# Twelve idle products, four slots for attention's inputs, and 350 GB/s in the ordering

## The chip, the cores and the metric

The kernel runs on one core of a Trainium2 chip. The metric is the device time of one execution in microseconds (us); less is better. Three executions of the kernel before took 841.60, 839.25 and 843.16 us, median 841.6.

## What is computed

Retention attention (a causal product without softmax, weighted by a decay for each head) feeds two feed-forward networks in a row. All inputs are f32 or f64, and the result is f32:

```
scores = q @ k.T / 8                       # 4 batches, 8 heads, 576 tokens, 64 wide
ret    = scores * gamma[h] ** (i - j)      # for i >= j, else 0
x      = (ret @ v), heads joined           # 2304 tokens x 512
h      = max(x @ w_in, 0);  x = (h*h) @ w_out          # 512 -> 2048 -> 512
out    = ((x @ w_a) * (x @ w_b)) @ w_out2              # 512 -> 1536 -> 512
```

The weights are 64-bit floats, which the kernel takes as pairs of 32-bit words and turns into f32 on the chip.

## The kernel before, in words

**Attention** (`attention`) runs in 20 units: for each batch four units of one pair of heads (seven blocks of 64 tokens each) and a fifth with the last two blocks of all four pairs. A unit's loads (`Unit.load`, DMA issued by SP) bring q and k into a slot of the ring `qkr` and v and k into a slot of `vr`, 448 KB each for most. A ring has `SLOTS[tag]` slots; a load into a slot waits for the last reader of the unit that had it. ScalarE scales k (`tv`, L615). A small table `vt` comes over ScalarE's own queue; one copy of a tile `first` on ScalarE (L594) stands behind it. `products` issues three steps per unit on TensorE: states (`tv`, `vr`), scores (`qkr`), and for the unit before it the sums (`pt`, `vr`, `qkr`, `sa`). All are f32 products of 64x64 tiles, 28 instructions for a step of 14 products: one f32 product is two MATMUL records. VectorE masks the scores and scans the states, ScalarE copies them.

**The MLPs** run on f32r halves: every f32 operand is split in a high and a low part, and three products are summed (hi*hi, lo*hi, hi*lo), 384 or 448 columns each. The first four chunks of the first network are done while attention is still under way (`mlps`: `up` and `down` steps, mixed with attention's units); the rest follows with a Strassen-like scheme of seven products (`rest`). Weights go from DRAM to a raw tile (`wraw`, or a part of `xt` lent for it), through two conversions on ScalarE and four on VectorE (`convert`), and most back to DRAM (`kept`). `bank` names the eight PSUM banks: `up` uses bank 7, only its second step uses bank 3, which is also the fourth accumulator of `down`.

**The order of the work** is written by a planner (`Plan`, L63 to L231). Every step is added with its engines and their costs in ns, the keys that it reads and writes, and a function that emits it. `order` first gives each step a latest time from the running sum of TensorE's costs (`ideal`), then runs twelve rounds of a greedy simulation forward (`forward`: on each free engine the ready step with the least latest time begins, at once if there is one) and one backward that renews the latest times. The best round's sequence is emitted, and each engine, SP's DMA queue too, then works through its own instructions in that order on the chip; a wait blocks what is behind it on its engine. Three numbers of the model matter here: a transfer costs its bytes divided by 310 per ns (at least 620 ns, `dmac`) on one single resource, free from 600 ns on, and lands 2100 ns later; TensorE's costs count double before `COLD` = 9000 ns; and a step with a choice of VectorE or GpSimd is never begun on GpSimd. The function on top (`tile_retention_two_mlps`) fills the constant tiles on VectorE, adds the steps and emits them.

Of the kernel before, what the change touches and what calls it, by code (L numbers as in the profile page):

```python
# [11 lines left out]
F32 = mybir.dt.float32  # L12
# [10 lines left out]
P = 128  # L23
# [19 lines left out]
RUN, LAG = {1: 2, 2: 3}, {1: 1, 2: 2.5}  # L43
SEVENS = {(2, 0): [range(6, 12)], (2, 1): [range(0, 6), range(6, 12)], (2, 2): [range(0, 6), range(6, 12)], (1,0):[range(8,12)], (1,1):[range(8,12)], (1,2):[range(8,12),range(12,16)]}
AFTER = 0.0
SPAN = 0.8
MORE = (2, 0, 6)
PARTS = set()
# [2 lines left out]

WP, WE, RAWS = 2, 1, 2
SLOTS = dict(
    g=2, r=2, gh=2, qkr=3, vr=3, tv=2, pt=2, sa=2, wraw=2, ys=4,
)

ROUNDS = 12
# [5 lines left out]
class Plan:  # L63
# [3 lines left out]


    LAT = {"PE": 200, "DMA": 2100, "ACT": 160, "DVE": 150}
    COLD = 9000  # L70

    def __init__(self):
        self.steps = []
        self.writers, self.readers, self.users, self.before = {}, {}, {}, {}
        self.pe = 0.0

    def add(self, engines, fn, r=(), w=(), extra=(), lag=None):


        n = len(self.steps)  # L80
        deps = set(extra)
        for k in {k[:2] for k in (*r, *w)}:
            deps.update(self.before.get(k, ()))
            self.users.setdefault(k, []).append(n)
        for k in r:
            deps.update(self.writers.get(k, ()))
        for k in w:
            deps.update(self.writers.get(k, ()))
            deps.update(self.readers.get(k, ()))
        for k in w:  # L90
            self.writers[k], self.readers[k] = [n], []
        for k in r:
            if k not in w:
                self.readers.setdefault(k, []).append(n)
        ideal = None
        if "PE" in engines:
            self.pe += engines["PE"]
            ideal = self.pe

        locks = not any(k[0] == "bank" for k in r)  # L100
        self.steps.append((engines, fn, deps, ideal, locks, lag))
        return n
# [40 lines left out]
    def forward(self, late):  # L143

        n = len(self.steps)
        missing = [len(s[2]) for s in self.steps]
        ready_at = [0.0] * n
        ready = {e: [] for e in self.ENGINES}
        free = {e: 0.0 for e in self.ENGINES}
        free["DMA"] = 600.0  # L150
        coming = [(0.0, i) for i in range(n) if not missing[i]]
        spans, out = [None] * n, []
        now = 0.0
        while True:
            began = []
            while coming and coming[0][0] <= now:
                _, i = heapq.heappop(coming)
                for e in self.steps[i][0]:
                    heapq.heappush(ready[e], (late[i], i))
                if not self.steps[i][0]:  # L160
                    began.append((now, i, None))
            for e in self.ENGINES:
                while ready[e] and free[e] <= now:
                    _, i = heapq.heappop(ready[e])
                    if spans[i] is None and not (e == "POOL" and "DVE" in self.steps[i][0]):
                        cold = e == "PE" and now < self.COLD
                        free[e] = now + self.steps[i][0][e] * (2 if cold else 1)
                        spans[i] = now, free[e], e
                        began.append((free[e], i, e))
                        break  # L170
            for end, i, e in began:
                if e is None:
                    spans[i] = now, now, None
                out.append((now, i, e))
                for j in self.follow[i]:
                    ready_at[j] = max(ready_at[j], end + self.lag(i, e, j))
                    missing[j] -= 1
                    if not missing[j]:
                        heapq.heappush(coming, (ready_at[j], j))
            times = [t for t in free.values() if t > now]  # L180
            if coming:
                times.append(max(coming[0][0], now))
            if not times:
                break
            now = min(times)
        assert len(out) == n, (len(out), n)
        return out, now, spans
# [54 lines left out]
def tile_retention_two_mlps(  # L242
# [12 lines left out]
    V, A, G, T = nc.vector, nc.scalar, nc.gpsimd, nc.tensor  # L255
    plan = Plan()

    def mm(o, l, r, start, stop):
        T.matmul(o, l, r, start=start, stop=stop, skip_group_check=True)  # L259
# [10 lines left out]
    def add(o, a, b):  # L270
        return lambda e: eng[e].tensor_add(o(), a(), b())  # L271
# [5 lines left out]
        return lambda e: nc.sync.dma_start(out=o(), in_=i())  # L277

    def dmac(bytes_):
        return {"DMA": max(620.0, bytes_ / 310.0)}  # L280

    big = ctx.enter_context(tc.tile_pool(name="big", bufs=1))
    dram = ctx.enter_context(tc.tile_pool(name="dram", bufs=1, space=bass.MemoryType.DRAM))
# [2 lines left out]
    bank = [psum.tile([P, 512], F32, name=f"bank{i}") for i in range(8)]  # L286
# [26 lines left out]
    ap = st.enter_context(tc.tile_pool(name="attn", bufs=1, side="right"))  # L313
# [22 lines left out]
    V.memset(fade[:, :, ::LONG], 0.0)  # L336

    V.memset(mask, 1.0)
    first = ap.tile([P, 2], F32, name="first")
    V.memset(first, 0.0)  # L340

# [123 lines left out]
    def keep_pair(ph, c, src):  # L465

        w, kw = slot("wp")
        a, b = [kw + (0,)], [kw + (1,)]
        convert(lambda: w[:, 512:1536], a + b, src, 1024)
        combine(w, add, 0, 4, 5, b, a)  # L470
        combine(w, sub, 1, 0, 2, [], a)
        combine(w, sub, 4, 2, 4, a, b)
        combine(w, sub, 6, 3, 1, a, b)
        keep((ph, c, 0), lambda: w[:, :1024], a, 1024)
        keep((ph, c, 1), lambda: w[:, 1024:1792], b, 768)

    def keep_outs(ph, c, src):

        w, kw = slot("wp")
        a, b = [kw + (0,)], [kw + (1,)]  # L480
        convert(lambda: w[:, 512:1536], b, src, 1024)
        if any(c in r for k, rs in SEVENS.items() if k[0] == ph for r in rs):
            combine(w, add, 0, 3, 5, b, a)
            combine(w, sub, 6, 2, 3, b, a)
            combine(w, sub, 1, 0, 2, b, a)
            combine(w, sub, 7, 4, 1, b, a)
            keep((ph, c, 4), lambda: w, a + b, 2048)
        else:
            keep((ph, c, 4), lambda: w[:, 512:1536], b, 1024)
# [437 lines left out]
    def rest():  # L927
# [113 lines left out]
        for ph in (1, 2):  # L1041
            for p in range(PASSES):
# [3 lines left out]
                while cs:  # L1046
                    run = next((list(r)[::2] for r in sevens if cs[0] in r), None)
                    if run:
                        run = [c + i for c in run[::1 - 2 * (p % 2)] for i in range(2)]
                        k = max(at[ph, p, c] for c in run if (ph, p, c) in at) + 1  # L1050
                        jobs.append(("sevens", ph, p, run, len(run) * 21 / 12, k + AFTER, None, cs[0] == begin))
                        cs = cs[len(run):]
# [17 lines left out]
        for x, job in enumerate(jobs):  # L1070
            nxt = jobs[x + 1][5] if x + 1 < len(jobs) else job[5] + 99
            if job[0] == "sevens":
                jobs[x] = job[:6] + (min(nxt, job[5] + SPAN * len(job[3]) / (2 if job[1] == 1 else 1)),) + job[7:]
            elif job[6] > nxt:
# [72 lines left out]
        def group(unit, banks, fresh):  # L1147
# [11 lines left out]
            for i, q, s, b, start in PRODUCTS:  # L1159
# [26 lines left out]
                elif i == 4:  # L1186
                    c12, k12 = take(tfree)
                    plan.add({"DVE": dve(n)}, add(c12, lambda: o[2], p5), [ko[2], k5], [k12])
                    tfree.append((p5, k5))
                    if ph == 2:  # L1190
                        plan.add({"DVE": dve(n)}, mul(c12, c12, c22), [k22], [k12])
                        tfree.append((c22, k22))
                    else:
                        relu({"ACT": act(n)}, c12, k12, c12, k12)
                        square((ph, p, 1, c), c12, k12)
                elif i == 5:
                    c22, k22 = take(tfree)
                    plan.add({"DVE": dve(n)}, add(c22, lambda: o[3], p5), [ko[3], k5], [k22])
                    if ph == 1:
                        relu({"ACT": act(n)}, c22, k22, c22, k22)  # L1200
                        square((ph, p, 1, c + 1), c22, k22)
                elif ph == 2:
                    plan.add({"DVE": dve(n)}, mul(c11, lambda: o[3], c11), [ko[3]], [k11])
                    for j, (g, kg) in enumerate(((c11, k11), (c12, k12))):
                        if unit in sevened:
                            made[ph, p, j, c] = g, kg
                            continue
                        gh, kgh = take(gfree)
                        plan.add({"ACT": act(n)}, copy(lambda gh=gh: gh()[:, 0], g), [kg], [kgh + (0,)])
                        lower((ph, p, j, c), gh, kgh, g, kg)  # L1210
                else:
                    c21, k21 = take(tfree)
                    relu(pa, c21, k21, lambda: o[3], ko[3])
                    square((ph, p, 0, c + 1), c21, k21)
# [201 lines left out]
        for _ in downs:  # L1416
            pass

    att = attention()
    while env["done"] < READY[0]:  # L1420
        next(att)
# [86 lines left out]
```

## Time and profile before

| | |
|---|---|
| median of three executions | 841.6 us (839.25 to 843.16) |
| the profiled execution | 843.72 us, of which the span from first to last instruction is 842.0 us |
| TensorE matmul (PE) busy | 823.7 us, 98% |
| VectorE (DVE) busy | 760.7 us, 90% |
| ScalarE (ACT) busy | 592.2 us, 70% |
| mean granted clock of TensorE | 0.994 |
| moved by DMA | 165.48 MB, mean 197 GB/s |

A view of stretches gives, for each stretch in us from the span's start: its length, then for each engine the busy time and the number of instructions (x), the granted TensorE clock (1.00 is 2.4 GHz, 0.50 is 1.2 GHz), the busy share of the DMA engines and GB/s. PEld is the load of stationary operands, which overlaps PE. The view of waits gives engine, operand and line, what ended the wait, and total us, times, longest us; "issue" means that the profile shows nothing that was waited for. The timeline gives start, us, engine, line, operation, out<-in, tile, count, and in brackets the idle time before it and what ended that. Line 259 is the helper that issues every product, line 277 the one that issues every DMA on SP. q8 is a DMA queue of the kind "instruction". A few per cent of the matmul records can be missing.

### The profile page before, as it was taken

The numbers are of one execution on the slowest core, as the hardware profiler recorded it, in microseconds if no ns is written. First come the engines' busy times: TensorE is split into PE (matmuls) and PEld (weight loads), VectorE is DVE, ScalarE is ACT, GpSimd is POOL, SyncE is SP. The second block draws the span as 40 slices with busy tenths as digits, with TensorE's granted clock in tenths as the row PEclk, the third lists the DMA queues.
The fourth block names the chain that finished last, engine by engine and source line by source line (L and its number), as shares of the span: only waits on it lengthen the run. The fifth ranks groups of instructions, "written<-read, shape, count | busy, mean of one in ns | idle before, by whom it ended". The sixth has DMA issues, their size and how long they took to land.

```text
span 842.0 us, 16895 instructions
## 1 busy us (share of the span) xinstructions
PE 823.7 (98%) x6516; PEld 801.0 (95%) x6516; DVE 760.7 (90%) x1280; ACT 592.2 (70%) x1074; POOL 0.7 (0%) x6
## 2 busy tenths in 40 slices
PE   6799999999999999999999999999999999999998
PEld 6687888999999999999999999999999999999998
DVE  7898899979999999999999999999887798797777
ACT  5687769788977798778985667566566566566554
POOL 0000000000000000000000000000000000000000
PEclk9899999999999999999999999999999999999999
DMA  8878958897437772586345688624544324544324
GB/s 284 307 248 271 333 195 331 300 335 241 134 138 276 256 256 75 204 293 223 102 144 193 216 289 301 213 65 136 172 136 136 109 63 127 174 139 139 106 73 130
DMA packets 67713, 165.48 MB, mean 197 GB/s; under 512 B 7216, under 2 KB 32048, under 8 KB 64560
## 3 DMA queue, kind: packets, MB, share of 16 engines
q1 hardware_dynamic: 67488, 164.39, 58.4%
q8 instruction: 51, 0.84, 0.4%
q14 instruction: 30, 0.25, 0.1%
q10 hardware_dynamic: 144, 0.01, 0.0%
HBM read 126.88 MB, written 37.49 MB: 195 GB/s over the span
## 4 chain that ended last, share of the span: by engine, by line
PE 91%; DVE 3%; DMA 2%; ACT 2%; issue 1%; ACTq 0%; DVEq 0%
PE bank L259 91%; DVE w L268 1%; DMA w<-kept 1%; DMA qkr<-qk 1%; DMA vt<-vtab 0%; ACT wp L390 0%; DVE xt L271 0%; ACT we L416 0%; ACT tv L615 0%; DVE wp L409 0%; ACT xb L265 0%; ACT w L265 0%; DVE wp L268 0%; ACT bank L265 0%; DVE wp L420 0%
## 5 line engine op out<-in xcount | busy, mean ns | idle before, releaser
L259 PE MATMUL bank<-xo,w 128*128 128x384 f32 x1946 | 395.8, 334 | 0.9 <-ACT bank L265 0.9
L259 PEld LDWEIGHTS bank<-xo,w 128*128 128x128 f32 x1946 | 342.2, 188 | 1.8 <-ACT bank L265 1.6
L259 PE MATMUL bank<-xb,w 128*128 128x384 f32 (+3 forms) x918 | 200.9, 347 | 0.8 <-ACT r L845 0.8
L268 DVE TENSOR_TENSOR w<-w 128x512 fp32r<-128x512 f32 (+3 forms) x193 | 166.7, 872 | 11.6 <-ACT w L265 11.1
L265 ACT CAST w<-w 128x512 fp32r<-128x512 f32 (+3 forms) x193 | 145.9, 769 | 37.8 <-DMA w<-kept 37.6
L259 PEld LDWEIGHTS bank<-xb,w 128*128 128x128 f32 x918 | 163.1, 189 | 8.1 <-ACT r L845 1.2
L259 PE MATMUL bank<-gh,w 128*128 128x384 f32 (+3 forms) x606 | 135.8, 349 | 0.4 <-ACT bank L265 0.4
L259 PEld LDWEIGHTS bank<-gh,w 128*128 128x128 f32 x606 | 107.8, 188 | 7.3 <-ACT bank L265 0.7
L265 ACT COPY bank<-bank 128x384 f32<-128x384 f32 x144 | 67.0, 466 | 55.9 <-PE bank L259 43.2
L259 PE MATMUL bank<-w,w 128*128 128x384 f32 x474 | 105.0, 334 | 0.0
L271 DVE TENSOR_TENSOR xt<-bank,xt 128x384 f32<-128x384 f32 (+1 forms) x142 | 83.0, 594 | 6.3 <-PE bank L259 5.4
L259 PEld LDWEIGHTS bank<-w,w 128*128 128x128 f32 x474 | 84.1, 188 | 0.1
L259 PE MATMUL bank<-ghl,w 128*128 128x384 f32 x372 | 80.5, 334 | 0.0
L259 PEld LDWEIGHTS bank<-ghl,w 128*128 128x128 f32 x372 | 65.8, 188 | 0.4 <-DVE xt L271 0.4
L420 DVE CUSTOM_DVE_ANT_0 wp<-wp,we 128x2048 uint16<-128x2048 uint16 (+1 forms) x35 | 41.7, 1190 | 0.3 <-ACT we L416 0.2
L268 DVE TENSOR_TENSOR wp<-wp 128x256 f32<-128x256 f32 (+1 forms) x86 | 36.2, 424 | 0.1
L268 DVE TENSOR_TENSOR xo<-xt,xo 128x768 fp32r<-128x768 f32 x36 | 34.1, 959 | 0.0
L390 ACT ACTIVATE wp<-raw 128x1024 f32<-128x1024 f32 x24 | 27.5, 1145 | 6.5 <-DVE xt L265 2.9
L265 ACT CAST xo<-xt 128x768 fp32r<-128x768 f32 x36 | 29.5, 834 | 3.1 <-PE bank L259 1.7
L416 ACT ACTIVATE we<-raw 128x1024 int32<-128x1024 uint32 x24 | 27.4, 1144 | 5.1 <-DVE wp L420 4.2
L409 DVE SCALAR_TENSOR_TENSOR wp<-raw,wp 128x1024 uint32<-128x1024 uint32 x24 | 29.3, 1221 | 0.1
L394 DVE TENSOR_SCALAR wp<-wp 128x1024 f32<-128x1024 f32 (+1 forms) x35 | 23.6, 674 | 3.6 <-ACT wp L390 3.6
(256 smaller groups left out, 968.1 us busy)
## 6 DMA issues: line engine op xcount, KB each, us to landing
raw<-w SPq DMA_DIRECT2D x24, 1024.0 KB, 6.1
w<-kept SPq DMA_DIRECT2D x46, 512.0 KB, 3.9
w<-kept SPq DMA_DIRECT2D x161, 128.0 KB, 3.0
w<-kept SPq DMA_DIRECT2D x46, 384.0 KB, 3.2
kept<-wp SPq DMA_DIRECT2D x20, 512.0 KB, 4.1
kept<-wp SPq DMA_DIRECT2D x10, 1024.0 KB, 4.8
wraw<-w SPq DMA_DIRECT2D x8, 1024.0 KB, 7.5
vr<-vk SPq DMA_DIRECT2D x16, 448.0 KB, 5.6
```

What stands on the lines that cost most here:

```text
L259: T.matmul(o, l, r, start=start, stop=stop, skip_group_check=True)
L265: return lambda e: A.copy(o(), i()) if e == "ACT" else eng[e].tensor_copy(o(), i())
L268: return lambda e: eng[e].tensor_sub(o(), a(), b())
L271: return lambda e: eng[e].tensor_add(o(), a(), b())
L390: {"ACT": act(n)}, lambda e: A.activation(like(w()), hi().bitcast(F32), AF.Abs), [kraw], kw
L394: lambda e: V.tensor_scalar(out=w(), in0=w(), scalar1=F64_MIN, scalar2=F64_MAX, op0=ALU.max, op1=ALU.min),
L409: lambda e: V.scalar_tensor_tensor(out=like(wu()), in0=hi(), scalar=0xC0000000, in1=like(wu()), op0=ALU.bitwise_and, op1=ALU.bitwise_or),
L416: lambda e: A.activation(like(rest[:, :n]), lo(), AF.Copy, scale=LO_ULPS), [kraw], [ke],
L420: lambda e: V._custom_dve(ADD32_U16LIMBS, out=w().bitcast(U16), in0=w().bitcast(U16), in1=rest[:, :n].bitcast(U16)),
```

## The change

A fill of a tile `calm` (128x256 f32) with zeros is added on VectorE, before that of `first`. Before any attention is planned, twelve steps on TensorE are added, each one f32 product of `calm` with itself (128x128 stationary, 256 columns) into bank 3, which nobody reads; as fillers they are left out of the running sum that gives the latest times, cost 440 ns each in the model, need only bank 3 and so follow one another, and the second `up` step is the next writer of that bank. The rings `qkr` and `vr` get four slots instead of three. In the planner a transfer costs its bytes over 350 and the doubled time of TensorE ends at 3400 ns. GpSimd may now begin a step with a choice if that step reads a bank (`steps[i][4]` is False for those alone).

```diff
--- before.py
+++ after.py
@@ -43,6 +43,7 @@
 RUN, LAG = {1: 2, 2: 3}, {1: 1, 2: 2.5}
 SEVENS = {(2, 0): [range(6, 12)], (2, 1): [range(0, 6), range(6, 12)], (2, 2): [range(0, 6), range(6, 12)], (1,0):[range(8,12)], (1,1):[range(8,12)], (1,2):[range(8,12),range(12,16)]}
 AFTER = 0.0
+CALM = 12
 SPAN = 0.8
 MORE = (2, 0, 6)
 PARTS = set()
@@ -51,7 +52,7 @@
 
 WP, WE, RAWS = 2, 1, 2
 SLOTS = dict(
-    g=2, r=2, gh=2, qkr=3, vr=3, tv=2, pt=2, sa=2, wraw=2, ys=4,
+    g=2, r=2, gh=2, qkr=4, vr=4, tv=2, pt=2, sa=2, wraw=2, ys=4,
 )
 
 ROUNDS = 12
@@ -67,14 +68,14 @@
 
 
     LAT = {"PE": 200, "DMA": 2100, "ACT": 160, "DVE": 150}
-    COLD = 9000
+    COLD = 3400
 
     def __init__(self):
         self.steps = []
         self.writers, self.readers, self.users, self.before = {}, {}, {}, {}
         self.pe = 0.0
 
-    def add(self, engines, fn, r=(), w=(), extra=(), lag=None):
+    def add(self, engines, fn, r=(), w=(), extra=(), lag=None, filler=False):
 
 
         n = len(self.steps)
@@ -93,7 +94,7 @@
             if k not in w:
                 self.readers.setdefault(k, []).append(n)
         ideal = None
-        if "PE" in engines:
+        if "PE" in engines and not filler:
             self.pe += engines["PE"]
             ideal = self.pe
 
@@ -162,7 +163,7 @@
             for e in self.ENGINES:
                 while ready[e] and free[e] <= now:
                     _, i = heapq.heappop(ready[e])
-                    if spans[i] is None and not (e == "POOL" and "DVE" in self.steps[i][0]):
+                    if spans[i] is None and not (e == "POOL" and "DVE" in self.steps[i][0] and self.steps[i][4]):
                         cold = e == "PE" and now < self.COLD
                         free[e] = now + self.steps[i][0][e] * (2 if cold else 1)
                         spans[i] = now, free[e], e
@@ -277,7 +278,7 @@
         return lambda e: nc.sync.dma_start(out=o(), in_=i())
 
     def dmac(bytes_):
-        return {"DMA": max(620.0, bytes_ / 310.0)}
+        return {"DMA": max(620.0, bytes_ / 350.0)}
 
     big = ctx.enter_context(tc.tile_pool(name="big", bufs=1))
     dram = ctx.enter_context(tc.tile_pool(name="dram", bufs=1, space=bass.MemoryType.DRAM))
@@ -336,6 +337,8 @@
     V.memset(fade[:, :, ::LONG], 0.0)
 
     V.memset(mask, 1.0)
+    calm = ap.tile([P, 256], F32, name="calm")
+    V.memset(calm, 0.0)
     first = ap.tile([P, 2], F32, name="first")
     V.memset(first, 0.0)
 
@@ -1416,6 +1419,10 @@
         for _ in downs:
             pass
 
+    for _ in range(CALM):
+        plan.add(
+            {"PE": 440}, lambda e: mm(bank[3][:, :256], calm[:, :P], calm, True, True), w=[("bank", 3)], filler=True
+        )
     att = attention()
     while env["done"] < READY[0]:
         next(att)
```

## Rows read from the trace of the kernel before

**Rows 1.** Page part 1: busy us, share, instructions of each engine.
```profile
PE 823.7 (98%) x6516; PEld 801.0 (95%) x6516; DVE 760.7 (90%) x1280; ACT 592.2 (70%) x1074; POOL 0.7 (0%) x6
```

**Rows 2.** View of stretches: us, busy of each engine, clock, DMA share, GB/s.
```profile
5.20:9.30 4.10, 4.08 (x72) 3.89 (x74) 3.28 (x8) 1.54 (x3) 0.00 (x0) 1.00 0.95 346
...
13.95:15.80 1.85, 0.00 (x1) 0.00 (x1) 1.85 (x4) 0.74 (x2) 0.00 (x0) 1.00 1.02 403
...
16.20:19.55 3.35, 3.35 (x47) 2.98 (x43) 1.42 (x3) 2.71 (x4) 0.00 (x0) 0.50 0.46 132
...
30.65:34.30 3.65, 0.00 (x0) 0.00 (x0) 1.87 (x2) 2.13 (x3) 0.00 (x0) 0.86 0.75 263
34.30:40.05 5.75, 5.75 (x116) 4.88 (x116) 4.72 (x7) 3.29 (x5) 0.00 (x0) 0.50 0.77 277
...
64.00:840.00 776.00, 773.07 (x5288) 755.92 (x5288) 708.17 (x1194) 548.92 (x1004) 0.00 (x0) 1.00 0.57 190
```

**Rows 3.** View of waits: who waited for whom, us in total, times, longest.
```profile
ACT w L265 <- DMA w<-kept: 37.6, 33, 3.3
...
PE bank L259 <- issue: 5.9, 3, 3.7
...
PE bank L259 <- DMA qkr<-qk: 1.3, 2, 0.8
```

**Rows 4.** Timeline of the start: VectorE's fills, ScalarE's first scaling, two of PE's steps.
```profile
3.10 0.27 DVE L336 MEMSET fade<- 128x256 f32 x1 [0.31 <-DVE fade L335]
...
4.49 0.67 ACT L615 ACTIVATE tv<-vr,vt 128x448 f32<-128x448 f32 x1 [0.82 <-DMA vt<-vtab]
...
5.21 1.76 PE L259 MATMUL bank<-tv,vr 64*64 64x64 f32 x28 [5.21 <-ACT tv L615]
...
9.73 0.81 PE L259 MATMUL bank<-qkr 64*64 64x64 f32 x22
```

**Rows 5.** View of stretches within attention's products.
```profile
5.50:9.00 3.50, 3.49 (x66) 3.30 (x64) 2.85 (x8) 1.25 (x2) 0.00 (x0) 1.00 0.94 339
10.00:12.00 2.00, 2.00 (x88) 2.00 (x84) 2.00 (x4) 1.83 (x4) 0.00 (x0) 1.00 1.01 379
16.50:18.00 1.50, 1.50 (x34) 1.50 (x32) 0.22 (x1) 1.31 (x2) 0.00 (x0) 0.50 0.12 42
28.60:30.60 2.00, 1.99 (x117) 1.96 (x118) 1.82 (x4) 1.83 (x3) 0.00 (x0) 1.00 0.87 298
```

**Rows 6.** Timeline of PE: two neighbouring groups of attention, two of the MLP.
```profile
21.99 0.98 PE L259 MATMUL bank<-qkr 64*64 64x64 f32 x28
22.91 0.87 PE L259 MATMUL bank<-xb,w 128*128 128x448 f32 x3
...
430.70 2.24 PE L259 MATMUL bank<-xo,w 128*128 128x384 f32 x12
432.78 0.68 PE L259 MATMUL bank<-w,w 128*128 128x384 f32 x3
```

**Rows 7.** Page part 3 (packets, MB, share), then stretches up to each gap.
```profile
q8 instruction: 51, 0.84, 0.4%
...
0.00:13.95 13.95, 8.51 (x222) 8.05 (x222) 9.76 (x21) 7.26 (x12) 0.67 (x6) 1.00 0.86 313
...
0.00:34.00 34.00, 21.69 (x603) 19.91 (x604) 25.57 (x47) 19.98 (x33) 0.67 (x6) 0.94 0.85 299
```

**Rows 8.** DMA queues within 13.5 to 13.625, 17 to 17.5, 32 to 32.125 us.
```profile
q8 instruction: 1, 0.02, 53.5%
...
q8 instruction: 1, 0.02, 12.0%
...
q8 instruction: 1, 0.02, 44.0%
```

**Rows 9.** SP: timeline of the fourth unit's first load; waits within 0 to 40.
```profile
11.45 0.34 SPq L277 DMA_DIRECT2D vr<-vk  x1
...
SPq L277 <- PE bank L259: 27.2, 11, 5.9
```

## The prediction, made before the change was run

> **What bounds the kernel now.** I read the busy shares first: TensorE (PE) is busy 823.7 of 842.0 us [rows 1], so the whole kernel is bound by TensorE and 18.3 us is all the idle time there is to win. Then the stretches: from 64 to 840 us PE is busy 773.07 of 776.00 us [rows 2], 2.9 us idle. What is left lies in the first 64 us, where attention's inputs and the first weights arrive, and it is of three kinds. PE does nothing before 5.21 us [rows 4]. It works at half pace: the granted clock is 0.50 from 16.20 to 19.55 and from 34.30 to 40.05 us, while PE is busy throughout [rows 2]. And it stands still in two gaps, 13.95 to 15.80 and 30.65 to 34.30 us, in which the view of waits names no releaser ("issue", longest 3.7 us) [rows 2, 3].
>
> The column of the granted clock reads 1.00 from the start, but the pace says otherwise: between 5.5 and 9.0 us 66 of attention's products take 3.50 us, 53 ns each; between 16.5 and 18.0, where 0.50 is granted, 44 ns each; between 10 and 12 us at 1.00, 23 ns [rows 5]. So the first products run at 1.2 GHz until about 9.3 us, some 4.1 us after the first one, and at 2.4 GHz from there. At half pace PE loses half its time: 2.05 us up to 9.3, 1.7 in the second stretch, 2.9 in the third.
>
> The two gaps look like the arrival of PE's own instructions. The instruction queue q8 moves 51 packets, and PE has 2 x 6516 records [rows 1, 7]: 255.5 a packet, or 128 products with their weight loads. PE has done 222 products at the first gap and 603 at the second [rows 7], 381 apart: 762 records, 2.98 packets. A packet is moved at 13.5 us and one at 32.0 [rows 8], and PE goes on 2.3 us after each. Counting 128 products back from a gap, a block was begun at about 10 us (72 products by 9.30, [rows 2]) and at about 28.1, so its successor took 3.5 to 3.9 us to be moved while the transfers ran at 400 GB/s [rows 2], but at most 1.7 us after 15.80, in a lull of 132 GB/s [rows 2, 8]. A block that PE empties in less than about 6 us ends in a gap under that load. With an MLP product at 173 ns (12 in 2.08 us, [rows 6]) 128 products take 22 us and nothing shows; attention's 117 took 2.00 us [rows 5].
>
> The Trainium skill ("Runtime: NRT & Kernel Launch", Instruction fetch mechanics) also has blocks of 256 instructions, fetched ahead, and calls the cost of crossing one "mostly hidden". The trace agrees on the size and not on "hidden". By that section of the Trainium skill the gaps would be waits for something else; that is the third rival.
>
> **The change, part by part.**
>
> *The zeroed tile.* One more fill on VectorE, 128x256, before the fill of `first`: 0.27 us by the row of that size [rows 4]. ScalarE's first copy and the mask wait 0.27 us more; ScalarE stands idle 0.82 us after its copy until the table of decays lands [rows 4], which hides it: cost nothing; without that cover 0.27.
>
> *The twelve products, first share.* They need only that tile, so on the chip they can start at about 3.4 (end of the fills before it, [rows 4]) + 0.3 = 3.7 us, not at 0 as the ordering thinks. It sees 440 ns each, doubled before 3400: 0, 880, 1760, 2640, 3520, then 3960, 4400, 4840. Its first real product there needs a transfer of 458,752 bytes at 350 (1.31 us) from 0.6, 2.1 us of lag and ScalarE's 0.62 + 0.16: 4.8 us. So I count seven ahead of it. Their price on the chip: no row shows this shape. From below 256 columns at the 0.451 ns of a column of an MLP product [rows 6], one pass: 0.12 us. Attention's f32 products show 28 records in 0.92 us [rows 6]; two records are one product and two products run side by side, so 0.131 us for 64 columns, 0.53 for 256. I take 0.5 at full clock, 1.0 at half (the upper end), as the rows are of the same type.
>
> Seven from 3.7 us: if the pace rises 4.1 us after the first product, as it did, that is 7.8 us, with four done; three more end at 9.3. Then 84 records, those that PE had before by 9.7 us (three steps of 28, the fourth starting at 9.73, [rows 4]), take 3 x 0.92 = 2.8 us at full pace: 12.1 against 9.7. **+2.4 us**, all on the path, as everything after hangs on these products. The bounds: none ahead -0.8 (the pace doubles 1.5 us earlier and nothing is delayed), twelve ahead (eight at full clock from 7.8) +4.9.
>
> *The other five.* They sit wherever the plan has a hole before the second up product, which is next on that bank. On the chip holes lie elsewhere. 0 to 5 x 0.5 = 2.5 us; one on the path, as the plan's holes are mostly PE's: **+0.5**. Behind the last queue the bank's next product; it came after 34 us and waits for nothing.
>
> *Four slots for attention's inputs.* The fourth unit's loads now stand behind a release: SP issues the first at 11.45 us and has waited 27.2 us for PE in the first 40 [rows 9]. They move to about 5 us, ahead of a weight load of 1 MB on SP; 0.9 MB at 403 GB/s [rows 2] puts that weight 2.2 us back. Attention's products hide it (PE has those), 2.2 if not; I take 0. What they can win on PE directly is its waits for these inputs, two, 1.3 us [rows 3]: **-1.3**. What is late next is the instruction packet.
>
> *350 for 310 GB/s, 3400 for 9000.* Both alter only the order. The loaded stretch moved 403 GB/s [rows 2], so 350 is nearer to the first 30 us than 310; from 64 us on, at 190, neither binds. From 64 us on there are 2.9 us to win at most; one late weight that comes through costs up to 3.3 us (33 waits of ScalarE, all hidden now, [rows 3]). I take 0 and keep -2.5 to +3.3. The new condition on GpSimd's choice alters nothing: no step offered to GpSimd reads a bank.
>
> *The gaps.* Twelve products are 24 product records, 19% of a block, so each block ends 24 real products earlier. Before the second gap that puts the request about 1.0 us earlier (across the wait ahead of 28.6 us) and the end of the block 24 x 17 ns = 0.4 earlier: -0.6. Loads spread further ahead leave less queued at 28 us; of the 2.2 us between 3.9 and 1.7 I take most, -1.4. **-2.0** together, half clock behind it unchanged, as the shorter gap of 1.85 us was followed by one too. Bounds: 0 gap and no half clock behind either, -1.85 - 1.7 - 3.65 - 2.9 = -10.1; another gap like the first, +3.5.
>
> The sum: 2.4 + 0.5 - 1.3 - 2.0 = -0.4 us on the profiled execution's 843.72, which stands 2.1 above the median of the runs (841.6). So **841.2 us**, no change that can be told: 0.5% (4.2 us) is about what a measurement of this kernel can tell from none, and the three runs spread over 3.9.
>
> **The rivals.**
>
> *The second gap goes, with its half clock* (faster). If the block ends inside MLP products, 173 ns each, the packet is there in time: -6.5 in place of -2.0, so -4.9: 836.7; with the first and its half clock gone too 833.1. For it: only one block in three ended in a gap. Against: attention's units come back to back until about 31 us whatever the order, and earlier inputs pack them more closely.
>
> *The feed falls behind* (slower). The place is 16 to 28 us: the two blocks there lasted about 6 us each, because of half clock and of waits. At full clock and with inputs at hand such a block is done in 4 us, less than the 6 of a packet under load, and a third gap opens. The gains are gone (0 for -3.3), the start stays (+2.9), and a gap like the first with its half clock comes on top (+3.5): +6.4, 848.0. It decides from 1.5 us of new gap on. For it: the pace of [rows 5]. Against: the block's packet in the lull came in 1.7 us.
>
> *The gaps are input waits* (much faster). Were they transfers that the profile doesn't tie to PE, a fourth slot would end both, with the half clock: 2.9 - 1.3 - 10.1 = -8.5, 833.1. The sentence of the Trainium skill quoted above points there. Against: PE stops within steps whose first products had run on the same operands, and the count of 2.98 packets.
>
> *The idle products don't do what they say.* If the pace rises at 9.3 us however early PE starts, seven take until 10.0: +3.1 for +2.4, 841.9. For it: from 34.30 us PE was busy 5.75 us before the clock rose, more than the 4.1 of the start [rows 2].
>
> **How the numbers follow.** Forecast 0.33, idle products without effect 0.12: both within 0.5%, 0.45. Second gap gone 0.23, gaps as input waits 0.10: faster, 0.33. Feed behind: slower, 0.22. The range goes from 833, where both faster cases end, to 847, short of the slower case's own end: it leaves out somewhat under 1 in 10 below and 1 in 10 above, and takes in the bounds of the order.
>
> **What would show it.** Right: seven or so f32 128x256 products from 3.7 us; the first attention product near 9.3 at a full pace; 84 records by about 12.1; no wait of PE for attention's inputs; the second gap at 1 to 2.5 us, an instruction packet about 2.3 us before its end. Wrong: products of attention before 6 us, or twelve idle ones ahead of them; a third gap between 16 and 28 us; no gap at all; idle time of PE past 64 us other than about 3 us.

## The result and the profile after

The changed kernel takes 853.35 us (median of four, 849.35 to 854.58) against 841.17 of before (four, 839.25 to 843.16): ratio 1.0127, 95% interval 1.0098 to 1.0155. It is slower by 12 us by the medians (10.7 by the ratio). The range had ended at 847, and "no change" was the forecast.

The first part of the page: busy time, share of the span and instructions of each engine.

```profile
PE 833.2 (98%) x6540; PEld 804.7 (94%) x6540; DVE 761.2 (89%) x1284; ACT 590.5 (69%) x1071; POOL 0.7 (0%) x6
```

TensorE (PE) is busy 833.2 us, 9.5 more than in [rows 1], though only 24 records were added. The idle time has hardly changed (18.5 us for 18.3). So "busy" hides the loss: the records of neighbouring products overlap (in [rows 6] the group from 430.70 lasts to 432.94, and the next starts at 432.78), so that a short wait between two products can show as nothing. The count of products done in a stretch shows it.

The timeline of the start, as in [rows 4]:

```profile
3.42 0.27 DVE L341 MEMSET calm<- 128x256 f32 x1
...
3.75 5.20 PE L260 MATMUL bank<-calm 128*128 128x256 f32 x14 [3.75 <-DVE first L343]
...
8.88 1.03 PE L260 MATMUL bank<-tv,vr 64*64 64x64 f32 x28
9.74 1.80 PE L260 MATMUL bank<-qkr 64*64 64x64 f32 x56
11.61 1.03 PE L260 MATMUL bank<-pt,vr 64*64 64x64 f32 x28
```

Fourteen records are seven idle products, from 3.75 us; attention's first product follows at 8.88, and after its first 84 records the next one starts at 11.61, for 9.73 before [rows 4]. In this execution the start went as forecast.

Stretches of the changed kernel (columns as in [rows 2]): the two gaps of the first 64 us, then the stages after 100 us.

```profile
15.27:17.30 2.03, 0.00 (x1) 0.00 (x0) 0.37 (x1) 2.03 (x4) 0.00 (x0) 1.00 1.04 406
...
35.00:37.10 2.10, 0.04 (x1) 0.00 (x0) 2.10 (x4) 2.10 (x3) 0.00 (x0) 1.00 0.88 343
...
120.00:140.00 20.00, 19.32 (x140) 15.82 (x139) 17.82 (x28) 14.91 (x23) 0.00 (x0) 1.00 0.33 95
140.00:200.00 60.00, 59.02 (x329) 55.11 (x328) 56.77 (x92) 50.55 (x87) 0.00 (x0) 1.00 0.97 348
200.00:600.00 400.00, 397.40 (x2279) 394.33 (x2279) 387.64 (x658) 299.48 (x551) 0.00 (x0) 1.00 0.57 193
```

The same three stages of the kernel before:

```profile
120.00:140.00 20.00, 20.00 (x90) 16.52 (x89) 19.69 (x31) 18.18 (x30) 0.00 (x0) 1.00 0.80 284
140.00:200.00 60.00, 59.97 (x344) 57.52 (x343) 54.13 (x89) 47.12 (x85) 0.00 (x0) 1.00 0.83 285
200.00:600.00 400.00, 399.14 (x2299) 398.25 (x2299) 390.89 (x665) 300.88 (x554) 0.00 (x0) 1.00 0.59 197
```

Between 200 and 600 us 2279 products were done for 2299: 20 x 0.173 us [rows 6] is 3.5 us that the busy columns put at 1.7. And the transfers have another shape. Between 120 and 140 us the DMA engines are busy a third of the time, where they had been at 0.80; then they run at 0.97 up to 200 us.

Where the queue went idle shows on SP, which issues nearly all transfers in order (waits of SP within 110 to 142 us, then its timeline):

```profile
SPq L278 <- DVE wp L269: 23.6, 4, 17.1
...
114.67 18.32 SPq L278 DMA_DIRECT2D kept<-wp  x3
...
133.22 0.38 SPq L278 DMA_DIRECT2D raw<-w  x1
```

SP stands 17.1 us at a write of converted weights whose conversion VectorE has not finished, and the next load of raw weights, behind it, goes out at 133.22. In that part the longest wait of before was 4.8 us:

```profile
SPq L277 <- DVE wp L409: 8.0, 2, 4.8
```

Such a wait alone is not a loss: further on, before has one of 14.5 and one of 17.3 us (between 200 and 400 us), and no stall there. What follows in the changed kernel's full queue, one stall as an example (timeline):

```profile
168.71 0.57 SPq L278 DMA_DIRECT2D w<-kept  x1
...
178.80 1.05 ACT L266 CAST w<-w 128x1024 fp32r<-128x1024 f32 x1 [1.34 <-DMA w<-kept]
...
179.88 1.23 DVE L269 TENSOR_TENSOR w<-w 128x1024 fp32r<-128x1024 f32 x1 [1.14 <-ACT w L266]
...
181.16 1.01 PEld L260 LDWEIGHTS bank<-xo,w 128*128 128x128 f32 x6 [0.90 <-DVE w L269]
```

A load of 512 KB issued at 168.71 lands at 178.78, 10.07 us later (median of its kind 3.7); ScalarE, VectorE and PE wait one after the other. Over the whole kernel (view of waits):

```profile
ACT w L266 <- DMA w<-kept: 55.0, 47, 3.6
...
ACT wp L393 <- DMA kept<-wp: 14.8, 13, 5.0
```

The first was 37.6 us in 33 waits [rows 3], the second 5.8 in 3. What TensorE itself waits for past 100 us shows on its weight loads (view of waits, the changed kernel, then before):

```profile
PEld bank L260 <- ACT bank L266: 5.4, 8, 1.3
...
PEld bank L259 <- ACT bank L265: 2.2, 3, 0.8
```

The longest entry in both is ScalarE's copy of a bank; the example of 350 alone below shows how a late weight holds that copy up.

To compare many kernels I use one sum, called **stalls past 100 us** below: from the timeline's single products, what the distance from one MLP product's start to the next exceeds the first one's pace (columns / 2.4 ns + 13), added up where it is over 60 ns. It is 3.2 us before and 9.8 after. With the same paces, PE's lag behind unbroken work grew between the two kernels by some 3 us up to 100 us and by some 6 more up to 838.

### The profile page after: what moved, and what is told of

It is laid out like the page before. It is cut to its first block, busy times and chain, and to the rows that moved or that the text cites. A ratio compares the mean times of both kernels' runs of the same rounds, so it can differ in the third digit from the quotient of the medians.

```text
span 851.7 us, 16929 instructions
## 1 busy us (share of the span) xinstructions
PE 833.2 (98%) x6540; PEld 804.7 (94%) x6540; DVE 761.2 (89%) x1284; ACT 590.5 (69%) x1071; POOL 0.7 (0%) x6
## 4 chain that ended last, share of the span: by engine, by line
PE 77%; DMA 8%; DVE 8%; ACT 4%; issue 2%; SPq 0%; ACTq 0%; DVEq 0%
PE bank L260 77%; DMA w<-kept 6%; DMA kept<-wp 2%; DVE wp L412 1%; DVE w L269 1%; ACT wp L393 1%; DVE wp L423 1%; DMA raw<-w 1%; ACT w L266 1%; DVE wp L269 1%; DVE xb L269 1%; ACT we L419 1%; DVE wp L397 0%; DVE sc L724 0%; SPq L278 0%
## 5 line engine op out<-in xcount | busy, mean ns | idle before, releaser
L260 PE MATMUL bank<-xb,w 128*128 128x384 f32 (+3 forms) x918 | 204.2, 348 | 2.4 <-DVE xt L272 0.8
L269 DVE TENSOR_TENSOR w<-w 128x512 fp32r<-128x512 f32 (+3 forms) x193 | 166.0, 869 | 17.3 <-ACT w L266 17.1
L266 ACT CAST xo<-xt 128x768 fp32r<-128x768 f32 x36 | 29.6, 835 | 1.1 <-DVE xt L269 0.8
```

The costliest lines, as they stand in the source:

```text
L266: return lambda e: A.copy(o(), i()) if e == "ACT" else eng[e].tensor_copy(o(), i())
L269: return lambda e: eng[e].tensor_sub(o(), a(), b())
```

## The experiments

Times are medians; each ratio is to the kernel before, run beside it, with its 95% interval. Stalls and DMA shares are of the one profiled execution.

| ordering | us | ratio (interval) | stalls past 100 us | DMA share 120-140 | 140-200 |
|---|---|---|---|---|---|
| before: 310 | 841.2 to 842.5 | 1 | 3.2 | 0.80 | 0.83 |
| changed kernel | 853.35 | 1.0127 (1.0098-1.0155) | 9.8 | 0.33 | 0.97 |
| 350 alone | 850.73 | 1.0105 (1.0084-1.0126) | 8.1 | 0.46 | 0.95 |
| four slots alone | 841.28 | 0.9995 (0.9981-1.0009) | 1.7 | 0.78 | 0.89 |
| idle products and 3400 alone | 843.65 | 1.0023 (1.0003-1.0043) | 1.3 | 0.60 | 0.84 |
| seven idle products, order of before | 845.87 | 1.0051 (1.0033-1.0069) | 1.9 | 0.67 | 0.88 |
| changed kernel at 310 | 845.20 | 1.0042 (1.0029-1.0054) | 2.5 | 0.61 | 0.90 |
| 290 | 843.09 | 1.0011 (0.9997-1.0025) | 2.1 | 0.68 | 0.83 |
| 312 | 837.89 | 0.9963 (0.9944-0.9982) | 1.9 | 0.81 | 0.86 |
| 330 | 844.81 | 1.0038 (1.0024-1.0052) | 3.1 | 0.57 | 0.88 |
| 370 | 852.94 | 1.0127 (1.0099-1.0156) | 8.1 | 0.58 | 0.89 |
| 350, kept loads land 0.5 us later | 853.26 | 1.0126 (1.0102-1.0151) | 6.9 | 0.41 | 0.92 |
| 350 for raw loads and kept writes | 845.35 | 1.0060 (1.0034-1.0087) | 6.7 | 0.94 | 0.85 |
| 350 for kept loads | 845.37 | 1.0049 (1.0032-1.0067) | 2.5 | 0.60 | 0.89 |
| 350 for attention, sums, outputs | 843.26 | 1.0016 (0.9998-1.0035) | 1.6 | 0.73 | 0.87 |
| 350 for all but raw loads and kept writes | 842.03 | 0.9994 (0.9979-1.0009) | 1.6 | 0.77 | 0.88 |
| 350 for raw loads | 842.54 | 1.0001 (0.9983-1.0019) | 1.8 | 0.87 | 0.85 |
| 350 for kept writes | 842.35 | 1.0005 (0.9984-1.0026) | 0.9 | 0.84 | 0.89 |
| order of 350, half of the kept writes | 846.29 | 1.0053 (1.0035-1.0071) | 2.3 | 0.40 | 0.87 |
| order of before, half of the kept writes | 841.32 | 0.9997 (0.9980-1.0014) | 1.3 | 0.74 | 0.75 |

### The parts alone

```diff
-        return {"DMA": max(620.0, bytes_ / 310.0)}
+        return {"DMA": max(620.0, bytes_ / 350.0)}
```

> The kernel before with one number changed: the ordering counts 350 GB/s. Theory A (the rate: with transfers thought faster, ScalarE's casts of weights stand too early in its queue and block the PSUM copies that TensorE waits for): stalls of TensorE past 100 us of 8 to 10 us in all (before 3.2, changed kernel 9.8), ScalarE waits for landing weights over 50 us (before 37.6, changed 55.0), time 846 to 848. Theory B (any new order loses, whatever the number): the same, and the other two single parts lose as much. Theory C (the loss is made in the first 50 us by idle products and slots): 840 to 842, stalls past 100 us about 3.

850.73 us: 350 alone makes 9 of the 12 us, more than any theory had. Its stretches:

```profile
120.00:140.00 20.00, 20.00 (x137) 16.77 (x132) 18.82 (x29) 12.80 (x21) 0.00 (x0) 1.00 0.46 149
140.00:200.00 60.00, 58.56 (x326) 54.56 (x325) 56.98 (x92) 50.48 (x90) 0.00 (x0) 1.00 0.95 335
```

The lull and the full queue are there without idle products and slots. A stall further on, where the queue is no longer full (timeline; the first row is the load that ScalarE waits for):

```profile
543.99 0.32 SPq L277 DMA_DIRECT2D w<-kept  x1
...
548.76 1.05 ACT L265 CAST w<-w 128x1024 fp32r<-128x1024 f32 x1 [4.10 <-DMA w<-kept]
549.71 0.47 ACT L265 COPY bank<-bank 128x384 f32<-128x384 f32 x1
...
550.23 0.98 PE L259 MATMUL bank<-xo,w 128*128 128x384 f32 x4 [0.90 <-ACT bank L265]
```

The load lands at 548.68, 4.7 us after its issue. ScalarE waits 4.10 us for it, and the copy of a bank that PE needs next stands behind that cast in its queue: PE waits for the copy. The Trainium skill ("TensorE: Matmul & The Clock Gate", Architectural detail) calls ScalarE's queue strictly first in, first out; these rows agree.

Of the ten stalls over 0.15 us past 100 us in this profile, seven go back in this way, through the work in order on ScalarE or VectorE, to a transfer that landed 4.7 to 7.6 us after its issue.

```diff
-    g=2, r=2, gh=2, qkr=3, vr=3, tv=2, pt=2, sa=2, wraw=2, ys=4,
+    g=2, r=2, gh=2, qkr=4, vr=4, tv=2, pt=2, sa=2, wraw=2, ys=4,
```

> The kernel before with four slots for attention's inputs, nothing else. Theory A (the rate): 840 to 842, stalls past 100 us about 3 us. Theory B (any new order loses): 845 to 850, stalls past 100 us 8 us or more. Theory C (the first 50 us): 843 to 845, all of it before 50 us.

841.28 us: nothing gained and nothing lost.

The idle products and the doubled cost until 3400, without slots and rate (the diff of the change without those two lines):

> The kernel before with the twelve idle products and the doubled cost until 3400, at 310 GB/s and three slots. Theory A (the rate): only the price of the start, +2.4, so 843 to 844, stalls past 100 us about 3. Theory B (any new order loses): 847 to 852. Theory C (the first 50 us): 845 to 847, with 4 us more lost by 50 us and nothing more past 100.

843.65 us, with 1.3 us of stalls past 100 us: the price of the start and no more. The three single parts multiply to 1.0105 x 0.9995 x 1.0023 = 1.0123, against 1.0127 for all together. Theory C (the first 50 us) falls, and so does B (any new order loses): the orders of these two runs differ from before's on every engine, and their stalls are fewer.

```diff
     steps, total = plan.order()
+    for _ in range(7):
+        mm(bank[3][:, :256], calm[:, :P], calm, True, True)
     for _, i, e in steps:
```

> The kernel before in its own order, with seven idle products put ahead of the first product of TensorE and of nothing else. All theories: first attention product at 8.9 us in place of 5.2. If the start's delay stays to the end: +2.4, so 843.6. If waits in the first 64 us take it up: 841 to 842. Stalls past 100 us about 3 us in either case.

845.87 us, +4.1 against the +2.4 forecast. Its PE timeline:

```profile
3.74 6.31 PE L259 MATMUL bank<-calm 128*128 128x256 f32 x14 [3.74 <-DVE first L342]
9.98 1.03 PE L259 MATMUL bank<-tv,vr 64*64 64x64 f32 x28
```

In this execution the seven took 6.24 us, 0.89 each, at half pace to the last, for 5.13 in the changed kernel's. How soon the pace rose after the first product differed between the two profiles with the same seven in front: here the idle products bought nothing, and delayed everything.

> The changed kernel with the rate put back to 310 GB/s (idle products and four slots stay). Theory A (350 is what costs, 9 us alone): 842 to 845, ScalarE's waits for landing weights under 46 us, stalls past 100 us 1 to 4. Rival (the parts need each other, or any combination of new orders loses): 848 or more.

845.20 us, stalls 2.5: putting the rate back takes 8 of the 12 us away.

### Is it the rate, or one unlucky order?

Each of these changes only the number in the line above (330, 290, 312, 370).

> The kernel before with 330 GB/s in the ordering. Theory A (the thought landing comes too early, the more the higher the rate): between the two ends, 843 to 848, ScalarE's waits for weights between 37.6 and 46.4 us. Rival A2 (310 was a lucky order, the rate as such says nothing): anything, 845 to 851 as likely as 841.

> The kernel before with 290 GB/s in the ordering. Theory A (too early landings): no loss, 839 to 843, ScalarE's waits for weights at 37 us or less. Rival A2 (310 was a lucky order): a loss here as well, 845 to 851.

> The kernel before with 312 GB/s in the ordering, a change that says next to nothing of the chip but may alter the order. Theories A and A3: 840 to 844, the scatter that a new order alone brings. Rival A2 (310 was a lucky order): 845 or more.

> 370 GB/s in the ordering. Theory A (the higher the rate is thought, the more comes late): stalls past 100 us 8 or more, 850 to 858. Rival A2 (350 was an unlucky order): anything from 838 to 847.

844.81, 843.09, 837.89 and 852.94 us. From 290 to 330 the orders scatter within about 3 us either way, with 2 to 3 us of stalls; three different orders that reckon all transfers at 350 or more (350, 370, and 350 with the kept loads counted 0.5 us later) lose 9 to 12 us each. That is outside the scatter, so A2 (one unlucky order) falls as the explanation of 350. ScalarE's waits for kept weights, the measure that theory A had named, do not follow the loss: 46.4 us with 350 alone (over 50 expected), 45.3 with the idle products and 3400 alone, 39.7 at 290 (37 or less expected). 312 had not been expected to gain: it beats both kernels. The view of the core's span and mean granted clock:

```profile
core 0: 839.7 us, clock 1.000
```

Before's mean granted clock is 0.994: its two stretches at 0.50 [rows 2] are absent in this order's profile. That profiled execution (841.45 us) is the slowest of its ten, so why the median is 3.4 us better stays argued.

### Which transfers?

```diff
-                dma(lambda cols=cols: to()[1].bitcast(F32)[:, cols], lambda of=of: of), [r], l, ex,
+                dma(lambda cols=cols: to()[1].bitcast(F32)[:, cols], lambda of=of: of), [r], l, ex, lag=2600,
```

> The kernel before with 350 GB/s, and the loads of kept weights thought to land 2600 ns after their transfer instead of 2100: 0.5 us later than with 350 alone, 0.3 later than with 310 for 512 KB. Theory A1 (each weight's landing time is what is wrong, and ScalarE's cast behind it blocks): back to 841 to 844, ScalarE's waits for weights under 40 us. Rival A3 (the load of the whole transfer queue is what is wrong, so the delays pile up): 848 or more.

853.26 us. ScalarE's waits for kept weights fell to 35.7 us in 25, below before's, and nothing was gained: A1 falls. Writes of 512 KB now land after 6.3 us (median; 4.1 before, 5.2 with 350 alone), which pointed to the whole queue. In the next six `dmac` takes a rate, 350 for the kinds named and 310 for the rest (shown: the first, for raw loads and kept writes):

```diff
-    def dmac(bytes_):
-        return {"DMA": max(620.0, bytes_ / 310.0)}
+    def dmac(bytes_, rate=310.0):
+        return {"DMA": max(620.0, bytes_ / rate)}
...
-        plan.add(dmac(P * 8 * n), dma(plane, source), w=[kraw], extra=exr)
+        plan.add(dmac(P * 8 * n, 350.0), dma(plane, source), w=[kraw], extra=exr)
...
-        plan.add(dmac(P * 4 * n), dma(lambda: kept[name], of), r, [("kept", name)])
+        plan.add(dmac(P * 4 * n, 350.0), dma(lambda: kept[name], of), r, [("kept", name)])
```

> The kernel before, with 350 GB/s in the ordering only for the loads of raw weights and the writes of kept weights; 310 for the rest. Theory A3 (conversions are packed too tightly into a transfer queue that can't move them, their writes land late, and ScalarE and SP wait in order behind them): most of the 9 us, 847 or more, writes of 512 KB landing after over 5 us (before 4.1). Rival (the loads of kept weights are what comes late): 841 to 844.

> The kernel before, with 350 GB/s only for the loads of kept weights. Theory A3: 840 to 844. Rival (these loads): 846 or more, ScalarE's waits for them over 45 us.

> The kernel before, with 350 GB/s only for attention's inputs, the sums' round trip and the outputs. Theory A3: 840 to 844. Rival A2 (every new order loses by chance): any of these three may lose 5 us or more.

845.35, 845.37 and 843.26 us. In time the first two can't be told apart, and neither has most of the 9 us, as A3 had wanted. In stalls they differ: 6.7 us for the conversions' transfers, 2.5 for the kept loads, so that most of the latter's 4 us must lie in the first 100 us, where the orders scatter. ScalarE's waits for the kept loads fell to 29.6 us, where over 45 were expected if these loads were at fault. Hence the complement:

> 350 GB/s in the ordering for everything but the loads of raw weights and the writes of kept weights, which stay at 310. Theory A3 (the conversions' transfers are the ones that are packed too tightly): stalls past 100 us of 1 to 3, as all orders with those at 310 had, and 841 to 846, the rest being the scatter of the first 100 us. Rival (all transfers alike): 6 or more of stalls, 847 or more.

842.03 us, stalls 1.6. With the raw loads and the kept writes at 310, 350 for all else costs nothing. And each of those two alone:

> 350 GB/s in the ordering for the loads of raw weights alone, 1 MB each. Theory A4 (raw loads thought 0.4 us shorter pull the conversions ahead, which then write more than the queue moves): stalls past 100 us of 5 or more, 844 to 850. Rival A5 (the writes' thought end is what is wrong): 840 to 843, stalls 1 to 3.

> 350 GB/s in the ordering for the writes of kept weights alone. Theory A4 (the raw loads): 840 to 843, stalls 1 to 3 past 100 us. Rival A5 (the writes): stalls of 5 or more, 844 to 850, writes of 512 KB landing after over 5 us.

842.54 and 842.35 us, stalls 1.8 and 0.9: A4 and A5 both fall. It takes both, and with both the other transfers add to it (850.73 for all, 845.35 for these two).

The table also bounds what the lull and the full queue can explain. 350 for raw loads and kept writes has its 6.7 us of stalls without them (0.94, then 0.85), while 330 and the changed kernel at 310 have shares like those of 370 (0.57 and 0.88, 0.61 and 0.90, for 0.58 and 0.89) with 3.1 and 2.5 us of stalls for its 8.1. They are one way in which transfers come late, not the measure of the loss.

### Is it the transfers, or the order as such?

On the chip only half of each kept weight is written and read back twice; the ordering counts it whole, so every engine keeps its order (shown: the write; the change of the reading side is left out).

```diff
-        plan.add(dmac(P * 4 * n), dma(lambda: kept[name], of), r, [("kept", name)])
+        plan.add(dmac(P * 4 * n), dma(lambda: kept[name], lambda: of()[:, :n // 2]), r, [("kept", name)])
```

> 350 GB/s in the ordering and, on the chip, only half of each kept weight written (the first half of its columns, read back twice where all is wanted); every engine's order is that of the kernel with 350 alone. Theory A (the transfers are slower than the ordering thinks, and what stands in order behind them stalls TensorE): with half of the writes gone most of the loss goes, 842 to 846, stalls past 100 us 4 or less. Rival A2 (the order itself is poor, whatever the transfers take): 849 to 851, stalls as with 350 alone, 8.

> The same halved writes in the order of the kernel before. The control: its transfers are hidden, so 839 to 842, stalls past 100 us 2 to 3. If it gains more than 3 us, the halved writes speed any order, and the run with 350 has to be read against that.

846.29 and 841.32 us. In the order of 350 half the writes bring 4.4 us back, in that of before nothing. The stretches of the first:

```profile
120.00:140.00 20.00, 20.00 (x144) 16.54 (x144) 19.50 (x33) 13.79 (x21) 0.00 (x0) 1.00 0.40 135
140.00:200.00 60.00, 60.00 (x338) 56.75 (x336) 58.82 (x96) 51.32 (x90) 0.00 (x0) 1.00 0.87 304
```

The lull is still there (0.40), but the queue after it is no longer full (0.87 for 0.95), PE is busy 60.00 of 60 us for 58.56, and the stalls past 100 us fall from 8.1 to 2.3. As the order is the same, each product's start can be set beside its start with 350 whole: with half the writes it is 2.7 us later at 100 us, level at 200 us (0.06 later), and 3.3 us earlier at the end, gained between 400 and 800 us. So up to 200 us the missing stalls make good an earlier delay, and whether the emptier queue took them away is not shown. The gain behind that, 3.3 us in the profiles and 4.4 in the medians, is what these bytes cost in the order of 350: a third to a half of its 9 us is made by transfers that take longer than the ordering allows, shown by taking bytes away. The other 4.6 us of this run lie in the first 100 us, by its stalls, and why is open.

## Why the prediction was wrong

**The step that failed** is the one on the rate: "Both alter only the order. [...] I take 0 and keep -2.5 to +3.3." It measured +9.0 us alone. It failed in three places.

Its premise, "from 64 us on, at 190, neither binds", took a mean for every stage. The 190 GB/s are those of 64 to 840 us [rows 2]; within them the transfers of before were near full for a time (view of stretches):

```profile
80.00:100.00 20.00, 20.00 (x435) 16.35 (x436) 16.11 (x27) 14.81 (x26) 0.00 (x0) 1.00 0.97 320
```

Its centre rested on "350 is nearer to the first 30 us than 310", by the 403 GB/s of [rows 2]. That stretch only loads. Where loads, raw weights and writes mix, a share of 0.97 moved these 320 GB/s, and 348 in the changed kernel between 140 and 200 us. An ordering that reckons with 350 plans there as if next to nothing were lost to waiting. The Trainium skill ("DMA: Bandwidth & Descriptors", Bandwidth) has 341 GB/s for a load of 1 MB and 425 for one of 16 MB, measured on one core. The 403 of loads alone lies between them; no run here varies the size of a load.

Its upper bound priced one late weight, 3.3 us. The runs show eleven stalls of 0.16 to 1.15 us past 100 us, 7.0 us together, in place of four, 2.0 together. One of them lies in the lull and three, 1.5 us, in the full queue, where loads land up to 10 us after their issue. The other seven come after 370 us; six of these are waits for ScalarE's copy of a bank, as in the example of 350 alone. A late transfer was priced singly, where many come late by less. "From 64 us on there are 2.9 us to win at most" was right and said nothing about what there was to lose. PE's idle time there, a sign of being wrong if it was not about 3 us, is 5.4:

```profile
64.00:838.00 774.00, 768.61 (x5281) 747.75 (x5269) 703.31 (x1186) 546.78 (x996) 0.00 (x0) 1.00 0.56 188
```

**The start** held in this execution: seven idle products (counted 7), 3.75 us (3.7), first attention product 8.88 (9.3), the record after the first 84 at 11.61 (12.1) for 9.73, so +1.9 here for +2.4. With the other five, "one on the path", the forecast was +2.9; alone in the ordering it measured +1.9 (0.3 to 3.6 by its interval). But the rival that the idle products don't do what they say is nearer in three of four profiles. The records of idle products start 0.43 us apart at half pace and 0.22 at full. That change comes at about 7.6 us in the changed kernel (forecast 7.8), but at 9.0 with the idle products and 3400 alone, at 9.2 in the changed kernel at 310, and not within the seven in front of an unchanged order, which give way at 9.98; the rival had said 9.3. So it is in part luck that the changed kernel's profile met the forecast.

**Four slots**, forecast -1.3: 0.9995 (0.9981 to 1.0009) leaves room for -1.6 to +0.8, so no gain is shown. The waits of PE for attention's inputs did go from the changed kernel's profile, and others came. Within 0 to 100 us:

```profile
PE bank L260 <- DVE first L343: 3.7, 1, 3.7
PE bank L260 <- issue: 2.5, 2, 2.0
PE bank L260 <- DVE pt L706: 2.4, 2, 2.1
```

**The gaps**, forecast -2.0 with half clock unchanged: half clock did follow both (from 17.9 to 21.3 and from 38.4 to 45.2 us). The first gap was 2.03 us for 1.85, and it came after the same 222 records as before [rows 7], of which 14 are now idle products:

```profile
0.00:15.27 15.27, 11.45 (x222) 9.98 (x222) 7.81 (x18) 4.48 (x8) 0.67 (x6) 1.00 0.88 320
```

A packet of q8 is moved at 15.05, 2.3 us before its end. That fits a block of fixed length and not a wait for inputs. The second shrank from 3.65 to 2.07 us, but it is not the gap of the forecast: it comes after 633 records for 603, no packet of q8 is moved between 31.1 and 37.3 us, and the profile names a releaser for it (VectorE's `pt`). So the 1.6 us are near the forecast by luck. No run took the packets away, so that they make the first gap stays an inference from the counts.

**The slower rival** had the sign and the wrong place: a third gap at 16 to 28 us did not open. No rival had put the loss past 100 us.

## What to carry to other kernels

When an order is written by a planner, a constant of its model is an edit of the whole kernel: price it by the resource that is nearest to full in any stage (here 0.97 of the DMA engines), not by the stage where the new number looks truer. A rate in such a model is not the peak of the resource but what it delivers with queueing: 290 cost nothing here that can be told (1.0011, 0.9997 to 1.0025), 350 cost 9 us. Where an engine works in order, a transfer that comes late holds up what stands behind its reader, so price a late transfer by that queue, and count how many can come late.

## What the runs showed of the hardware

The time from PE's first product to the rise of its pace varied between profiles with idle products from 3.75 us on: about 3.9, 5.2 and 5.4 us in three, and over 6 in the fourth. A DMA share of 0.97 went with 320 GB/s in one stretch and with 348 in another. The profile's busy time of PE, 9.5 us more for the same useful products, took in the stalls that the count of products shows.
